# Folding the query weights early, in one burst, and keeping them in DRAM

## The chip, the cores and the metric

The kernel runs on one core of a Trainium2 chip. The metric is the time of one execution on the device in microseconds (us). A profiled execution also has a span, from its first to its last instruction, and a trace in which every instruction and transfer has its time.

## The reference

Two branches are computed from 2048 tokens of 512 features and mixed by a gate of each token.

```python
x = A_x                                         # 1 x 2048 x 512
g = sigmoid((x * gate_w).sum(-1))               # one gate per token
q, k, v = split(x @ wqkv)                       # 32 heads of 16
pq, pk = q @ w_phi[h], k @ w_phi[h]             # a 16 x 16 matrix per head
phi = concat([softmax(p), softmax(-p)])         # for pq and for pk
kv, z = phi_k^T v, sum over tokens of phi_k
a = (phi_q kv) / (phi_q z + 1e-6) @ wo
b = relu(x @ w1 + b1)^2 @ w2 + b2               # inner width 1792
out = g * a + (1 - g) * b
```

Since `pq = x @ (wq_h w_phi[h])`, the kernel multiplies each head's `wq` by its `w_phi` once (it folds them) and then projects the tokens with the folded weights. The same is done for the keys. The query fold is what is changed here.

## The kernel before

Tokens are cut into 4 blocks of 512 and each block into 4 chunks of 128. The feed-forward branch runs in two sweeps over the blocks. A sweep takes 7 of the 14 inner tiles of 128 features: for each block and inner tile one `up` (12 matmuls of 512 columns into one PSUM bank) and one `down` (12 matmuls, three into each of the four banks `d`). A float32 product is made of three matmuls with high and low parts (`mm3`, L76 to L78).

Everything else is hung between these matmuls by hand. `work_list` has 56 entries, and entry t owns the half steps 2t, 2t + 0.5, 2t + 1 and 2t + 1.5: before `up`, in its middle, before `down` and in its middle. So half steps stand six matmuls apart, and `at(slot, f, ...)` puts a function on one of them. The order that results is a priority: a planner lays the instructions of each engine out by it ahead of time, and `tc.high_priority(offset=AHEAD)` moves one forward in it, `tc.issue_after(i)` keeps one behind another on its engine, `behind()` keeps one behind the latest work of ScalarE and VectorE on `up`. On the chip each engine runs its own list in order and waits for semaphores.

What the change touches:

- `load_fold` (L141) loads `w_phi` and the four row tiles of `wqT` into five buffers of the pool `row`, which has six (`row`, L89). The same pool holds the token rows of the gate (`gate_load`, L265), the parts that the first sweep writes to DRAM at the end of each block (`part`, L898 to L910) and `kv_room`.
- `query_fold(half)` (L191) at half steps 51.5 and 53: 32 matmuls each, by `fold_block` (L166), over array tiles of 32 x 32 with 128 columns, into two PSUM banks; then VectorE transposes each bank in 32 x 32 blocks (`turned`, L174) and ScalarE and VectorE split the result into high and low parts (L63, L66), the weights `wq` of the projection `q` from half step 56.5 on.
- `tiles_fold` (L177) is the same fold for the keys, at half step 5.5.
- `pair_steps(p, s)` (L660) computes keys and values of two chunks by seven products, blocks 1 to 7 (`run(i)`, L680), with three sums of weights that are reloaded from DRAM (`wkeep`, `again`, L644) by ScalarE's queue. Pair 0 starts at s = 14, pair 1 at 18.5. Blocks 1, 6, 5, 3 write the bank X (pool `ps_e`), blocks 2, 7, 4 the bank Y, from the rotating list `banks`. `place` (L675, L677) takes the results out of X on ScalarE, out of Y on VectorE; `place7` is that of block 7, and block 4 adds to the same bank behind it. `phi` then makes the exponentials of a chunk.
- At that time `banks` holds two pools, which `up` and Y share. `ps_b` belongs to the sums `kv` from half step 21.5 on.

Of the kernel before, what the change touches and what calls it, by code (L numbers as in the profile page):

```python
# [7 lines left out]
F32 = mybir.dt.float32  # L8
F32R = mybir.dt.float32r
AF = mybir.ActivationFunctionType  # L10
# [5 lines left out]
P = 128  # L16
S, D, H, DH, F = 2048, 512, 32, 16, 1792
NK = D // P
# [10 lines left out]
AHEAD = 150  # L29
# [5 lines left out]
def tile_gated_mix(ctx: ExitStack, tc: tile.TileContext, xT, xn, wqT, wkT, wphi, wv, wo, w1, b1, w2, b2, gw, out):  # L35
    nc = tc.nc
# [8 lines left out]
    dram = pool("dram", 1, space=DRAM)  # L45
    ps_d = pool("ps_d", NC, space=PSUM)
    ps_a, ps_b, ps_e, ps_f = (pool(f"ps_{i}", 1, space=PSUM) for i in "abef")
    banks = [ps_a, ps_b, ps_e, ps_f]
    def used(p):
        banks.remove(p)  # L50
        banks.append(p)

    def bank(name):
        p = banks[0]
        used(p)
        return p.tile([P, 512], F32, tag="s", name=name)
# [4 lines left out]
    def split(src, hi, lo, ehi, elo):  # L61
        if ehi is nc.scalar:
            i = nc.scalar.activation(hi, src, AF.Copy)  # L63
        else:
            i = ehi.tensor_copy(hi, src)
        st["lo"] = elo.tensor_tensor(lo, src, hi.bitcast(F32), ALU.subtract)  # L66
        return i
# [21 lines left out]
    def row():  # L89
        return work.tile([P, D], F32, tag="row", name="row", bufs=6)  # L90
# [29 lines left out]
    st, up_w, down_w = {}, {}, {}  # L120
# [8 lines left out]
    nc.gpsimd.tensor_tensor(kvb, kvb, kvb, ALU.add)  # L129
    part = dram.tile([NB * NC, P, D], F32, name="part")  # L130
    wkeep = dram.tile([len(KEPT), 2, P, 2 * D], F32, name="wkeep")
    zrow = dram.tile([2 * D], F32, name="zrow")
    vext = [hold.tile([P, H * VW], F32, tag="vz", name=f"vext{i}") for i in range(NV)]
    heads = lambda v: v.rearrange("p (h v) -> p h v", v=VW)
# [28 lines left out]
    def fold_block(loaded, out, g, r, c):  # L163
        wph, *t = loaded
        rows, cols = slice(32 * r, 32 * r + 32), slice(32 * c, 32 * c + 32)
        return nc.tensor.matmul(out[cols, g * P:(g + 1) * P], wph[rows, g * P + 32 * r:g * P + 32 * r + 32],  # L166
                                t[g][rows, :].rearrange("p (k c q) -> p k c q", c=4, q=32)[:, :, c, :],
                                start=True, stop=True, skip_group_check=True)

    def turned(pss, half):  # L170
        tb = work.tile([P, 2, 4, NK, 32], F32, tag="tb", name="turned", bufs=2)
        for r in range(2):
            with tc.high_priority(offset=AHEAD):
                st["turned"] = nc.vector.transpose(tb[:, r].rearrange("p g k q -> p (g k q)"), pss[2 * half + r])  # L174
        return tb

# [11 lines left out]
                    nc.scalar.activation(dst[:, h, 0, :, 2 * half:2 * half + 2],  # L188
                                         tb[:, :, 2 * h:2 * h + 2, k].rearrange("p r g q -> p g r q"), AF.Copy)

    def query_fold(half):  # L191
        pss = {r: bank(f"fold{r}") for r in (2 * half, 2 * half + 1)}
        for g, c, r in [(g, c, r) for g in range(NK) for c in range(4) for r in pss]:
            with tc.issue_after(st["up"].ins):
                st["up"] = fold_block(st["wT"], pss[r], g, r, c)
        tb = turned(pss, half)
        part_ = lambda t: t.rearrange("p (g r f) -> p g r f", g=NK, f=32)[:, :, 2 * half:2 * half + 2, :]
        for k in range(NK):
            if not half:
                st.setdefault("wa", []).append(tuple(  # L200
                    wpool.tile([P, 512], F32R, tag=f"wa{hl}{k}", name=f"wq{hl}{k}") for hl in "hl"))
            hi, lo = st["wa"][k]
            split(tb[:, :, :, k].rearrange("p r g q -> p g r q"), part_(hi), part_(lo), nc.scalar, nc.vector)
# [84 lines left out]
    def e_tile(tag="e"):  # L288
        if tag == "tmp":
            return st["tmp"][1].rearrange("p (h t f) -> p h t f", t=2, f=DH)  # L290
        return work.tile([P, H, 2, DH], F32, tag="e", name="e", bufs=2)
# [343 lines left out]
    def again(p, i, j):  # L635
        if i not in KEPT:
            return nullcontext()
        step = 2 * KEPT.index(i) + j
        nxt, t = step + 3, st["slots"][step % 3]
        if nxt >= 6 and p == LASTP:  # L640
            return nullcontext()
        k, jj = KEPT[nxt % 6 // 2], nxt % 2
        st["W"][k, jj] = both(t)
        return tc.issue_after(nc.scalar.dma_start(t.bitcast(F32), wkeep[KEPT.index(k), jj]).ins)  # L644
# [15 lines left out]
    def pair_steps(p, s):  # L660
        b, c = ROWS[p]
        n, m = b * NC + c, b * NC + c + 2
        v = {}

        def place(t, half, src, other=None):
            i = 2 * p + (t == m)
            if ("e", t) not in v:
                v["e", t] = e_tile("tmp" if i % NV == NV - 1 else "e")
                v["v", t] = vext[i % NV]
            hs = slice(16 * half, 16 * half + 16)  # L670
            to = (v["e", t][:, hs, 0, :], heads(v["v", t])[:, hs, :DH])
            for o, cols in zip(to, halves):
                of = lambda z: z[:, cols].rearrange("p (h f) -> p h f", f=DH)
                if other is None:
                    read = nc.scalar.activation(o, of(src), AF.Copy)  # L675
                else:
                    read = nc.vector.tensor_tensor(o, of(other), of(src), ALU.add)  # L677
            return read

        def run(i):  # L680
            first, other = i in (1, 2, 7), "Y" if i in (2, 7, 4) else "X"
            if i == 1:
                if p == 0:
                    banks.remove(ps_e)
                v["X"] = ps_e.tile([P, 512], F32, tag="s", name="pX")
            elif first:
                v["bank"] = banks[0]
                v["Y"] = bank("pY")
            elif i == 4:
                used(v["bank"])  # L690
            block(v[other], p, i, first)
            with tc.high_priority(offset=AHEAD), again(p, i, 0):
                if i in (1, 6, 5):
                    v[i] = st["tmp"][0][:, 512 * (i == 6):512 * (i == 6) + 512]
                    read = nc.scalar.activation(v[i], v["X"], AF.Copy)  # L695
                elif i == 7:
                    return
                else:
                    t, half, u = {2: (n, 0, 1), 3: (n, 1, None), 4: (m, 0, 6)}[i]
                    read = place(t, half, v[other], v.get(u))  # L700
            with tc.issue_after(read.ins):
                again(p, i, 1)

        def place7():
            with tc.high_priority(offset=AHEAD):
                place(m, 1, v["Y"], v[5])

        def phi(t):
            e3, r = exps(e=v["e", t])
            with tc.high_priority(offset=AHEAD):  # L710
                v["phi", t] = scaled(e3, r)

        def kv():
            if p == 0:
                st["kv"] = ps_b.tile([P, 2 * P], F32, tag="s", name="kvps")
            later = kv_chunk(p == 0, False, st["kv"], v["phi", m], v["v", m])
            with tc.issue_after(later.ins):
                st["up"] = kv_chunk(False, p == LASTP, st["kv"], v["phi", n], v["v", n])

        at(s - 2 - (p > 0), sums_load, p)  # L720
        if p == 0:
            at(s - 2, sums_add, p)
        at(s - 1.5 if p else s - 0.5, sums, p)
        for off, i in zip((0, 1, 1.5, 2, 2.5, 3, 4), (1, 2, 6, 5, 7, 3, 4)):
            at(s + off, run, i)
        if p == LASTP:
            at(s + 4, banks.append, ps_e)
        at(s + 3, place7)
        at(s + 3, phi, n)
        at(s + 4, phi, m)  # L730
        at(s + 7.5 + (p == LASTP) * 1.5, kv)
# [55 lines left out]
    SL = 2 * NFH  # L787
    steps = {}

    def at(slot, f, *a):  # L790
        steps.setdefault(int(2 * slot) / 2, []).append(lambda: f(*a))
# [9 lines left out]
        at(14.5, joint_last, j)  # L801
    for b in range(NB):
        for c in range(NC):
            s = b * SL + 2.5 * c - 1 if b > 1 else 17.5 + c / 2 if b else max(5.5, 3.5 + 2 * c)
            if b != 1 or c < 2:
                at(s, gate_load, b * NC + c)
            at(s + (4.5 if b == 1 else 3), gate_chunk, b * NC + c)
        if c == NC - 1:
            at(s + 4.5 if b == 1 else s + 3, gates, b)
        s, late = ((4, 2), (19.5, 1), (22, 2.5), (36, 2))[b]  # L810
        at(s, x_load, b + 1)
        for k in range(NK):
            at(s + late + k / 2, x_split, b + 1, k)
    for p in range(NB * NC // 2):
        pair_steps(p, 14 + 4.5 * p)
    base = (NB - 1) * SL
    at(49, do_wT, wqT)
    at(51.5, query_fold, 0)
    at(53, query_fold, 1)
    for k in range(NK):  # L820
        at(base + 8.5 + k, wo_load, k)
        at(base + 10 + k, wo_split, k)
# [10 lines left out]
    for p in range(NB * NC // 2):  # L833
        n, s = 2 * p, 56.5 + 6 * p
        q, late = divmod(n, NC)[0], p == NB * NC // 2 - 1
# [122 lines left out]
```

## Time and profile before

| | |
|---|---|
| median of 3 runs | 506.2 us (506.01 to 506.32) |
| the profiled execution | 506.27 us |
| its span | 504.5 us, 9559 instructions |
| busy: PE, PEld, DVE, ACT, POOL | 499.7, 403.9, 404.7, 259.9, 88.1 us |
| granted TensorE clock | 0.999 |
| DMA | 76.13 MB, mean 151 GB/s |

PE is TensorE's matmuls, PEld its weight loads, DVE VectorE, ACT ScalarE, POOL GpSimd, SP the engine that only issues transfers. A row of a timeline has the start in us, the duration in us, engine, line of the kernel, instruction, output <- inputs with shapes, and how many were merged; in brackets the idle time before it and what ended it. Matmuls overlap: 512 columns last 0.39 us each but start 0.23 us apart. A row of a line or tile has the shortest, median and longest duration in ns, and first and last start. A row of windows has the stretch, its length, the busy time and number of instructions for PE, PEld and further engines, and at its end the granted clock, the share of DMA in use and GB/s; where it is asked for one line alone, it counts only that line's instructions. "DMA to landing" is the time from a transfer's issue to the arrival of its last byte.

### The profile page before, as it was taken

What the parts mean: (1) busy time and instruction counts of PE and PEld (TensorE: products, weight loads), DVE (VectorE), ACT (ScalarE), POOL (GpSimd) and SP (SyncE); (2) the same over time, 40 slices, a digit from 0 to 9 for tenths busy, and PEclk for the clock granted to TensorE, in tenths of its full rate; (3) what the DMA queues carried; (4) which work ended last, traced back from release to release, by engine and by line L of the source; (5) the groups of instructions that cost most, each with busy time, mean ns of one, the idle gap of its engine ahead of it and who ended that gap; (6) DMA issues with size and microseconds to landing.
All of it is one profiled execution on the core that took longest, in us unless ns stands there. A gap on an engine that the chain in (4) does not pass through costs nothing.

```text
span 504.5 us, 9559 instructions
## 1 busy us (share of the span) xinstructions
PE 499.7 (99%) x3616; PEld 403.9 (80%) x3616; DVE 404.7 (80%) x680; ACT 259.9 (52%) x470; POOL 88.1 (17%) x103
## 2 busy tenths in 40 slices
PE   8999999999999999999999999999999999999997
PEld 5878788888888888888788878788787878788776
DVE  5569957799785969796988989897979796897724
ACT  4887655466263474453793644454455353333540
POOL 1000151204510025000012140212222221112200
PEclk9999999999999999999999999999999999999999
DMA  8858587666854578762167131324212221041112
GB/s 263 285 197 279 184 315 215 215 216 233 295 187 156 180 225 309 261 218 75 43 182 280 39 109 47 101 71 138 54 31 90 71 88 44 6 136 51 36 29 83
DMA packets 45830, 76.13 MB, mean 151 GB/s; under 512 B 6869, under 2 KB 23001, under 8 KB 45785
## 3 DMA queue, kind: packets, MB, share of 16 engines
q1 hardware_dynamic: 36072, 41.78, 26.5%
q10 hardware_dynamic: 6768, 23.79, 13.6%
q0 software_dynamic: 2944, 9.96, 5.4%
q8 instruction: 28, 0.46, 0.3%
q14 instruction: 18, 0.14, 0.1%
HBM read 57.68 MB, written 11.54 MB: 137 GB/s over the span
## 4 chain that ended last, share of the span: by engine, by line
PE 93%; DMA 3%; DVE 2%; issue 1%; ACT 1%; SPq 0%; ACTq 0%; DVEq 0%
PE d L76 9%; PE d L77 9%; PE d L78 9%; PE u L76 9%; PE u L77 9%; PE u L78 9%; PE pX L656 3%; PE q L78 3%; PE att L78 3%; PE att L76 3%; PE q L76 3%; PE att L77 3%; PE q L77 3%; PE pX L658 3%; PE pX L657 3%; PE pY L656 2%
## 5 line engine op out<-in xcount | busy, mean ns | idle before, releaser
L425 ACT ACTIVATE r<-u,b1c 128x512 f32<-128x512 f32 x56 | 38.5, 687 | 110.1 <-PE u L78 108.3
L76 PE MATMUL d<-w2h,hh 128*128 128x512 f32 x222 | 86.8, 391 | 0.0
L77 PE MATMUL d<-w2l,hh 128*128 128x512 f32 x222 | 86.4, 389 | 0.0
L78 PE MATMUL d<-w2h,hl 128*128 128x512 f32 x222 | 86.4, 389 | 0.0
L76 PE MATMUL u<-xh,w1h 128*128 128x512 f32 x212 | 83.5, 394 | 0.0
L77 PE MATMUL u<-xl,w1h 128*128 128x512 f32 x212 | 82.6, 390 | 0.0
L78 PE MATMUL u<-xh,w1l 128*128 128x512 f32 x212 | 82.5, 389 | 0.0
L337 POOL TENSOR_TENSOR ez<-e,z 128x512 f32<-128x512 f32 x32 | 43.0, 1366 | 164.1 <-ACT e L313 164.1
L66 DVE TENSOR_TENSOR hl<-r,hh 128x512 fp32r<-128x512 f32 x56 | 37.9, 677 | 22.9 <-ACT hh L63 22.9
L76 PEld LDWEIGHTS d<-w2h,hh 128*128 128x128 f32 x222 | 41.7, 188 | 9.6 <-issue 1.0
L76 PEld LDWEIGHTS u<-xh,w1h 128*128 128x128 f32 x212 | 39.8, 188 | 11.4 <-issue 2.9
L78 PEld LDWEIGHTS d<-w2h,hl 128*128 128x128 f32 x222 | 41.7, 188 | 8.7
L77 PEld LDWEIGHTS d<-w2l,hh 128*128 128x128 f32 x222 | 41.7, 188 | 8.5
L78 PEld LDWEIGHTS u<-xh,w1l 128*128 128x128 f32 x212 | 39.8, 188 | 8.4
L77 PEld LDWEIGHTS u<-xl,w1h 128*128 128x128 f32 x212 | 39.8, 188 | 8.0
L313 ACT ACTIVATE e<-e 128x1024 f32<-128x1024 f32 x27 | 28.6, 1060 | 32.5 <-DVE e L311 32.1
L295 DVE TENSOR_REDUCE sm<-e 128x64 f32<-128x1024 f32 x27 | 32.8, 1215 | 10.8 <-ACT e L313 10.8
L63 ACT ACTIVATE hh<-r 128x512 fp32r<-128x512 f32 x56 | 35.1, 627 | 1.0
L427 ACT ACTIVATE r<-r 128x512 f32<-128x512 f32 x56 | 34.9, 624 | 0.7
L378 ACT ACTIVATE phiT<-tb 32x256 f32<-32x256 f32 x64 | 26.4, 413 | 8.8 <-DVE tb L363 7.9
L695 ACT ACTIVATE tmp<-pX 128x512 f32<-128x512 f32 x24 | 14.4, 598 | 29.7 <-PE pX L658 24.7
L347 DVE TENSOR_REDUCE dz<-ez 128x64 f32<-128x1024 f32 x16 | 19.4, 1212 | 11.7 <-POOL ez L337 11.7
(181 smaller groups left out, 981.4 us busy)
## 6 DMA issues: line engine op xcount, KB each, us to landing
sloto<-wkeep ACTq DMA_DIRECT2D x30, 512.0 KB, 4.3
in<-in_xT SPq DMA_DIRECT2D x42, 256.0 KB, 4.4
slotez<-wkeep ACTq DMA_DIRECT2D x15, 512.0 KB, 6.0
phiT<-tb SPq DMA_DIRECT2D x192, 32.0 KB, 1.8
in<-in_w SPq DMA_DIRECT2D x23, 256.0 KB, 3.3
part<-row POOLq DMA_DIRECT2D x16, 256.0 KB, 5.2
row<-part SPq DMA_DIRECT2D x16, 256.0 KB, 3.2
out<-row SPq DMA_DIRECT2D x15, 256.0 KB, 2.2
```

What stands on the lines that cost most here:

```text
L63: i = nc.scalar.activation(hi, src, AF.Copy)
L66: st["lo"] = elo.tensor_tensor(lo, src, hi.bitcast(F32), ALU.subtract)
L76: nc.tensor.matmul(o, ah[:, sa], bh[:, sb], start=first, stop=False)
L77: nc.tensor.matmul(o, ah[:, sa], bl[:, sb], start=False, stop=False)
L78: return nc.tensor.matmul(o, al[:, sa], bh[:, sb], start=False, stop=last)
L295: nc.vector.tensor_reduce(sm, e3, AX.X, ALU.add)
L313: nc.scalar.activation(ef, ef, AF.Exp)
L337: nc.gpsimd.tensor_tensor(ez[:, hs, :], e3[:, hs, :], zbc[half], ALU.mult)
L378: nc.scalar.activation(dst, src, AF.Copy)
L425: st["relu"] = nc.scalar.activation(r, ps, AF.Relu, bias=b1c[:, fc:fc + 1])
L427: nc.scalar.activation(r, r, AF.Square)
L656: nc.tensor.matmul(ps, h, wh, start=first and j == 0, stop=False, skip_group_check=True)
```

## The change

The five loads go to half step 16. At 17.5 one burst of 16 matmuls of 512 columns, one for each pair of row group r and column group g of the array, folds all query weights into four banks: the two of `banks`, `ps_e` and `ps_b`. ScalarE copies each bank into a `row` buffer, and 16 transfers of 64 KB from SP's queue put them into the DRAM tensor `qkeep`. At half step 49 four loads of 256 KB bring them back, and at 51.5 and 53 `query_turn` does what `query_fold` did after its matmuls, with the transposes reading SBUF and not moved forward in priority. For the banks, pair 0 runs block 4 at half step 17 (18 before) and `place7` at 16.5 (17 before). The gate loads of block 1 go from 17.5 to 18.5, with their products.

```diff
+    qkeep = dram.tile([4, 4, 32, NK, P], F32, name="qkeep")
...
-    def turned(pss, half):
+    def turned(pss, half, ahead=True):
         tb = work.tile([P, 2, 4, NK, 32], F32, tag="tb", name="turned", bufs=2)
         for r in range(2):
-            with tc.high_priority(offset=AHEAD):
+            with tc.high_priority(offset=AHEAD) if ahead else nullcontext():
                 st["turned"] = nc.vector.transpose(tb[:, r].rearrange("p g k q -> p (g k q)"), pss[2 * half + r])
         return tb
...
-    def query_fold(half):
-        pss = {r: bank(f"fold{r}") for r in (2 * half, 2 * half + 1)}
-        for g, c, r in [(g, c, r) for g in range(NK) for c in range(4) for r in pss]:
-            with tc.issue_after(st["up"].ins):
-                st["up"] = fold_block(st["wT"], pss[r], g, r, c)
-        tb = turned(pss, half)
+    def query_fold():
+        pss = [p.tile([P, 512], F32, tag="s", name=f"fold{r}") for r, p in enumerate((banks[0], ps_e, banks[1], ps_b))]
+        wph, *t = st["wT"]
+        for g in range(NK):
+            for r in range(4):
+                rows, cols = slice(32 * r, 32 * r + 32), slice(32 * g, 32 * g + 32)
+                with tc.issue_after(st["up"].ins):
+                    st["up"] = nc.tensor.matmul(
+                        pss[r][cols, :], wph[rows, g * P + 32 * r:g * P + 32 * r + 32],
+                        t[g][rows, :].rearrange("p (k c q) -> p c k q", c=4, q=32),
+                        start=True, stop=True, skip_group_check=True)
+        for r in range(4):
+            t = row()
+            with tc.high_priority(offset=AHEAD):
+                st["folded"] = nc.scalar.activation(t, pss[r], AF.Copy)
+            for g in range(NK):
+                nc.sync.dma_start(qkeep[r, :, :, g, :].rearrange("c f x -> f c x"),
+                                  t[32 * g:32 * g + 32, :].rearrange("f (c x) -> f c x", c=4))
+
+    def query_load():
+        st["wT"] = [row() for _ in range(4)]
+        for r, t in enumerate(st["wT"]):
+            nc.sync.dma_start(t, qkeep[r].rearrange("c f g x -> (c f) (g x)"))
+
+    def query_turn(half):
+        tb = turned(st["wT"], half, False)
...
-        for off, i in zip((0, 1, 1.5, 2, 2.5, 3, 4), (1, 2, 6, 5, 7, 3, 4)):
+        for off, i in zip((0, 1, 1.5, 2, 2.5, 3, 4 if p else 3), (1, 2, 6, 5, 7, 3, 4)):
             at(s + off, run, i)
...
-        at(s + 3, place7)
+        at(s + (3 if p else 2.5), place7)
...
-            s = b * SL + 2.5 * c - 1 if b > 1 else 17.5 + c / 2 if b else max(5.5, 3.5 + 2 * c)
+            s = b * SL + 2.5 * c - 1 if b > 1 else 18.5 + c / 2 if b else max(5.5, 3.5 + 2 * c)
...
-    at(49, do_wT, wqT)
-    at(51.5, query_fold, 0)
-    at(53, query_fold, 1)
+    at(16, do_wT, wqT)
+    at(17.5, query_fold)
+    at(49, query_load)
+    at(51.5, query_turn, 0)
+    at(53, query_turn, 1)
```

## The prediction

> **What bounds the kernel now.** I read the page's head and chain first, then TensorE's timeline round the work that the change touches, then ScalarE, VectorE and DMA at the step where it goes.
>
> ```profile
> span 504.5 us, 9559 instructions
> PE 499.7 (99%) x3616; PEld 403.9 (80%) x3616; DVE 404.7 (80%) x680; ACT 259.9 (52%) x470; POOL 88.1 (17%) x103
> PE 93%; DMA 3%; DVE 2%; issue 1%; ACT 1%; SPq 0%; ACTq 0%; DVEq 0%
> 66.14 0.39 PE L76 MATMUL u<-xh,w1h 128*128 128x512 f32 x1
> 71.58 0.39 PE L656 MATMUL pY<-w,xh 128*128 128x512 f32 x1
> 57.45 0.40 PE L76 MATMUL u<-xh,w1h 128*128 128x512 f32 x1
> 57.96 0.50 PE L656 MATMUL pX<-slotez,sh 128*128 128x512 f32 x1
> ```
>
> TensorE is busy 99% of the span and is 93% of the chain, so time is what TensorE issues plus the places where its stream breaks. From 66.14 to 71.58 there are 24 matmuls: 5.44 us, 0.227 us each; that is the beat. The step from 57.45 to 57.96 misses it by 0.28 us: one of the few waits. A change gains here only by taking time out of TensorE's stream, and loses by every wait that it puts into it. Other engines' work is free as long as nobody in that stream waits for it.
>
> **What is removed.** Two query folds at half steps 51.5 and 53.
>
> ```profile
> 240.52 0.39 PE L78 MATMUL d<-w2h,hl 128*128 128x512 f32 x1
> 240.84 1.15 PE L166 MATMUL fold<-row 32*32 32x128 f32 x64
> 241.92 0.50 PE L76 MATMUL d<-w2h,hh 128*128 128x512 f32 x1
> 242.26 0.39 PE L77 MATMUL d<-w2l,hh 128*128 128x512 f32 x1
> 246.23 1.15 PE L166 MATMUL fold<-row 32*32 32x128 f32 x64
> ```
>
> The stream goes from 240.52 to 242.26 with two ordinary matmuls in it: 1.74 - 2 x 0.227 = 1.29 us for the burst with its switch in and out. The second burst has the same 64 passes and the same 1.15 us, so I put it at 1.29 too: 2.58 us leave the stream. (32 matmuls show 64 passes: float32 goes through twice.)
>
> **What is added on TensorE.** One burst of 16 matmuls, 32 passes of 512 columns, two in each of 16 array tiles. No such pass is in the trace; these rows bound it.
>
> ```profile
> L166 PE MATMUL fold<-row x256: 265/268/293, 26.6 to 247.1; 32*32 32x128 f32 x128
> L389 PE MATMUL num<-phiT,kvb x256: 376/376/400, 296.6 to 488.3; 64*32 64x256 f32 x128
> 296.28 0.39 PE L78 MATMUL u<-xh,w1l 128*128 128x512 f32 x1
> ...
> 296.59 1.09 PE L389 MATMUL num<-phiT,kvb 64*32 64x256 f32 x32
> 297.62 0.50 PE L76 MATMUL u<-xh,w1h 128*128 128x512 f32 x1
> 297.95 0.40 PE L77 MATMUL u<-xl,w1h 128*128 128x512 f32 x1
> 26.61 1.90 PE L166 MATMUL fold<-row 32*32 32x128 f32 x128
> 26.60:26.73 0.13, 0.12 (x16) 0.12 (x31) 1.00 0.68 205
> 246.20:246.34 0.14, 0.11 (x8) 0.11 (x16) 1.00 0.00 0
> ```
>
> A pass takes 268 ns with 128 columns and 376 ns with 256: 108 ns for each 128 columns, so 432 ns of streaming for 512. The key fold of the start, over 16 tiles, starts 16 passes in its first 0.13 us; the query fold, over 8 tiles, starts 8 in 0.14 us. So every tile streams at the same time as the others, and one tile's two passes are what follows each other. Streaming in the new burst is 2 x 432 = 0.86 us. The old query burst has 8 x 108 = 0.86 us of streaming in each tile and costs 1.29, so 0.43 us for the switches and the staggered starts; num has 4 x 216 = 0.86 us and costs 1.67 - 0.45 = 1.22, so 0.36. Lower bound of the new burst: 0.86 + 0.43 = 1.29 us. Upper bound: its passes arrive only as fast as in the key fold's whole burst, (1.90 - 0.27) / 127 = 12.8 ns apart, so the last tile starts 31 x 12.8 = 0.40 us late: 0.86 + 0.36 + 0.40 = 1.62 us. I take the upper one, since a bank that the third matmul writes comes free only just before the burst (below), so few passes can be queued ahead. Gain on TensorE: 2.58 - 1.62 = 0.96 us, and 1.29 at best.
>
> A rule of the Trainium skill speaks against this ("TensorE: Matmul & The Clock Gate", Part 3: Packing small matmuls): matmuls start and end strictly in program order. By it a tile's second pass would hold up the next tile. The two window rows, 16 and 8 starts at once, say otherwise for passes of this kind; what it would give is a rival below.
>
> **Moved earlier: place7 and block 4 of pair 0.** Block 4 ran at half step 18 from 71.58 on. It now follows block 3 at 17, so the burst is due 24 beats after 66.14 (six of `up`, block 3, block 4, six of `down`): at 71.58, where block 4 was.
>
> ```profile
> 70.08 0.68 DVE L309 TENSOR_REDUCE mn<-e 128x32 f32<-128x512 f32 x1
> 70.79 0.69 DVE L310 TENSOR_TENSOR e<-mn,e 128x512 f32<-128x512 f32 x1
> 73.14 0.42 DVE L677 TENSOR_TENSOR e<-tmp,pY 128x256 f32<-128x256 f32 x1 [0.93 <-PE pY L658]
> 66.40 0.42 DVE L677 TENSOR_TENSOR e<-tmp,pY 128x256 f32<-128x256 f32 x1 [2.67 <-ACT hh L63]
> ```
>
> place7's additions ran at 66.4 already, and block 4 now comes 12 beats after 66.14, at 68.86: nothing waits. Block 4's two additions of 0.42 us can follow mn at 70.8 and free the Y bank at about 71.5: in time by a tenth. If they came only after the next two steps of phi(n) (2 x 0.69), TensorE would stand for up to 1.4 us. I take 0, because these additions are issued ahead of phi(n) by priority. The X bank was last written by block 3, six beats earlier, and kv's bank is not in use yet.
>
> **Moved earlier: five loads (weights) to half step 16.** They need five of the six `row` buffers. Four hold block 0's parts then.
>
> ```profile
> 52.00:56.00 4.00, 4.00 (x19) 3.32 (x18) 4.00 (x11) 1.48 (x3) 0.93 (x2) 1.00 0.64 256
> 68.00:72.00 4.00, 4.00 (x19) 3.34 (x18) 2.45 (x4) 2.20 (x5) 2.46 (x5) 1.00 0.73 263
> 72.00:76.00 4.00, 4.00 (x19) 3.30 (x19) 3.07 (x7) 2.24 (x4) 0.00 (x0) 1.00 0.77 304
> L910 POOL DMA_DIRECT2D part<-row x1: 542/542/542, 63.4 to 63.4; - x1
> DMA to landing us min/median/max: 4.8/4.8/4.8
> L145 SPq DMA_DIRECT2D row<-in_wqT x4: 328/338/1360, 199.7 to 236.2; - x4
> DMA to landing us min/median/max: 3.1/4.4/8.6
> L265 POOL DMA_DIRECT2D row<-in_xn x2: 544/553/562, 68.3 to 68.9; - x2
> 56.11 0.60 ACT L695 ACTIVATE tmp<-pX 128x512 f32<-128x512 f32 x1 [1.47 <-DMA wkeep<-spare]
> 80.20 0.62 ACT L63 ACTIVATE xh<-in 128x512 fp32r<-128x512 f32 x1
> 81.10 0.39 PE L656 MATMUL pX<-slotez,sh 128*128 128x512 f32 x1
> ```
>
> Two loads find free rows before; the other three follow the first three part stores. The third store starts at 63.4 and lands 4.8 us later, at 68.2; the same load before took 3.1 to 8.6 us, so the last weights land at 71.3 to 76.8, 72.6 by the median. Its four matmuls are the last of the burst and due at about 72.0 (71.58 and three quarters of the paced starts). I take no wait, since the DMA share there is 0.73 and the two gate loads (xn) that ran at 68.3 and 68.9 now wait for rows themselves, until the burst frees them at about 73. Those two stand on GpSimd's queue, and the loads of token block 2 behind them; ScalarE first splits one of these at 80.20, so 4 to 5 us of delay leave some cover and cost nothing.
>
> **Added after the burst.** Four copies on ScalarE: the 0.60 us row above, 2.4 us from about 73 on. ScalarE has 1.8 and 1.76 us free in the two windows 68 to 76, and what stands behind them on ScalarE (the sums of pair 1) is first used at 81.10. The next `up` needs the first copy alone, one `down` group (1.36 us) after the burst: hidden. If that cover went, up to 2.4 us would show.
>
> ```profile
> 245.85 1.73 SPq L243 DMA_DIRECT2D in<-in_wo  x4
> 45.60 44.88 SPq L611 DMA_DIRECT2D in<-in_xT  x3
> L66 DVE TENSOR_TENSOR wql<-turned,wqh x8: 392/416/420, 248.1 to 254.2; 128x256 fp32r<-128x256 f32 x8
> 258.42 0.39 PE L76 MATMUL q<-wqh,xh 128*128 128x512 f32 x1
> ```
>
> Sixteen stores of 64 KB on SP: the nearest row, four pieces of 64 KB, issues one in 0.43 us: 6.9 us, 73 to 80, on a queue that issues three transfers between 45.6 and 90.5. They are hidden, since whatever SP does next comes after them; their 1 MB shares the DMA with the reloads of `wkeep`, at a share of 0.77. At half step 49 four loads replace five. The four transposes remain but no longer go ahead of other VectorE work; the last query weight was done by 254.7 and is used at 258.42, a cover of 3.7 us. I cost all this at 0.
>
> **Sum.** 506.27 us (the profiled execution; its span of 504.5 and 1.8 around it) - 2.58 + 1.62 + 0 = 505.31. The median of the runs, 506.20, is 0.07 lower, so the forecast is 505.2 us, 504.9 with the lower bound of the burst.
>
> **Rivals.**
> 1. The early loads collide. ScalarE waited 1.47 us at 56.11 for the store of `spare` to land, and TensorE's gap at 57.96 hangs on that queue. If the rows that block 0's last gate chunks free just before then are the ones used, a 256 KB load runs beside that store. At the 256 GB/s of 52 to 56 it takes 1.0 us; from nothing to 1.0 us goes into the gap. Time 505.2 to 506.2, 505.7 in the middle. The Trainium skill ("DMA: Bandwidth & Descriptors", Issuing engines are not separate DMA queues) says that transfers of all issuing engines share the same 16 DMA engines; no row here shows these two together.
> 2. The burst waits for its last weights, or is cut up by it (the slower side). At a landing of 76.8 it is 4.8 us late and the time 510.0; from 1.0 us late the gain is gone, from 2.0 us the kernel is slower by 0.2%. If the planned order puts other matmuls between, each further piece costs at least the switch and two streams, 0.36 + 0.86 = 1.2 us: in two pieces 506.5, in three 507.7. For it: five of six buffers, and stores in between. Against: the median landing is 0.6 us late at most.
> 3. Passes go in order: 17 x 0.432 + 0.36 = 7.7 us for the burst, 506.2 - 2.58 + 7.7 = 511.3. The starts of 16 and 8 at once are against it.
>
> **How the numbers follow.** A change of 0.2% (1.0 us) is about what a measurement of this kernel tells from none. Forecast (whole burst, all hidden, 504.8 to 505.5): 0.52, of which 0.40 beyond 0.2%. Rival 1: 0.26, of which 0.03 beyond it. Rival 2: 0.20, of which 0.02 within 0.2%. Rival 3: 0.02. So faster 0.43, same 0.37, slower 0.20. The range of 8 in 10 is 504.7 to 507.2: below, the best burst with a little of the old gaps gone; above, a burst in two to three pieces or 2 us late.
>
> **What would show it.** Right: no fold at 240 and 246; one group of 32 passes near 72 us, 1.3 to 1.6 us out of the beat; the step at 57.96 as before; later work earlier by 1 us after half step 53. Wrong: the group in several pieces with `d` or `u` between; TensorE released by a DMA of `row`; a longer gap at 58; `u` waiting for a fold copy on ScalarE; q waiting for `wql` after 254.

## The result and the profile after

The changed kernel takes 515.7 us (median of 5 runs, 514.8 to 515.9) against 506.2 before: ratio 1.018, 95% interval 1.017 to 1.020. It is slower by 9.5 us where 1.0 us less was forecast. The profiled execution after is the fastest of the five: 514.78 us, a span of 513.0. One execution is left out of the range and the ratio given for its kernel below: one of the five of experiment 8 took 1287.9 us at a granted clock of 1.00, and no trace of it was kept.

The head of the page after, with the granted clock, the DMA and the chain:

```profile
span 513.0 us, 9412 instructions
PE 502.6 (98%) x3520; PEld 404.1 (79%) x3520; DVE 407.7 (79%) x680; ACT 261.9 (51%) x474; POOL 86.0 (17%) x103
PEclk9999999999999999999999979999999999999999
PE 88%; DMA 4%; SPq 3%; DVE 3%; issue 1%; ACT 1%; ACTq 0%; DVEq 0%
```

There are fewer instructions, yet TensorE is busy 3 us longer and the granted clock has one weak slice, the 24th of 40, which is about 295 to 308 us. The chain has lost 5 points of PE to DMA, SP's queue and VectorE: TensorE now waits where it did not. TensorE's timeline after shows where, in order of time:

```profile
58.47 0.42 PE L679 MATMUL pX<-slotez,sl 128*128 128x512 f32 x1
60.65 0.50 PE L677 MATMUL pX<-sloto,sh 128*128 128x512 f32 x1 [1.75 <-DMA sloto<-wkeep]
...
73.04 0.39 PE L78 MATMUL d<-w2h,hl 128*128 128x512 f32 x1
73.36 1.38 PE L199 MATMUL fold<-row 32*32 32x512 f32 x32
74.66 0.50 PE L76 MATMUL d<-w2h,hh 128*128 128x512 f32 x1
75.00 0.39 PE L77 MATMUL d<-w2l,hh 128*128 128x512 f32 x1
...
75.93 0.40 PE L78 MATMUL d<-w2h,hl 128*128 128x512 f32 x1
76.87 0.50 PE L76 MATMUL u<-xh,w1h 128*128 128x512 f32 x1 [0.55 <-ACT row L206]
...
260.12 0.39 PE L76 MATMUL q<-wqh,xh 128*128 128x512 f32 x1
...
298.36 0.59 PE L410 MATMUL num<-phiT,kvb 64*32 64x256 f32 x2
301.91 1.96 PE L410 MATMUL num<-phiT,kvb 64*32 64x256 f32 x30 [2.96 <-DMA phiT<-tb]
303.79 0.79 PE L76 MATMUL u<-xh,w1h 128*128 128x512 f32 x1
304.38 0.63 PE L77 MATMUL u<-xl,w1h 128*128 128x512 f32 x1
```

Read each against the beat of 0.227 us (a row's start minus the start of the row above it):

- Near 58, a wait for the reload of `sloto`. All gaps of this place together are 1.76 us longer than before.
- The burst: 75.00 - 73.04 = 1.96 for the burst and two ordinary matmuls, so 1.51 us. Forecast: 1.29 to 1.62.
- `u` waits for the first fold copy: 0.72 + 0.11 = 0.83 us out of the beat.
- `num`, the first product of the first query pair, has two passes and then waits 2.96 us for `phiT`. Its other 30 passes take 1.96 us, where the whole of it took 1.09 before, and the matmuls behind stand 0.43 us apart instead of 0.227. Counted in the beat, this place is 6.54 us longer than before.

The windows of the kernel after, whose third number from the right is the granted clock, say what the 0.43 us are:

```profile
core 0: us, PE busy (x) PEld busy (x) DVE busy (x) ACT busy (x) POOL busy (x), PEclk, DMA share, GB/s
301.90:303.80 1.90, 1.89 (x31) 0.73 (x31) 1.83 (x3) 0.00 (x0) 1.35 (x2) 0.50 0.70 207
303.80:308.20 4.40, 4.40 (x16) 3.46 (x11) 4.37 (x6) 2.53 (x5) 0.00 (x0) 0.50 0.46 160
```

For some 6 us behind the wait TensorE ran at half clock. The whole account: -2.57 (old bursts) + 1.51 + 1.76 + 0.83 + 6.54 + 0.23 (a short wait near 133 that the kernel before doesn't have) = 8.3, and the two profiled executions are 514.78 - 506.27 = 8.5 apart.

Why is `phiT` late? VectorE transposes each chunk into `tb`, and SP sends 24 pieces, one after the other, for the two chunks of a pair. SP's rows of the kernel before:

```profile
279.32 15.39 SPq L372 DMA_DIRECT2D phiT<-tb  x24
```

and of the kernel after:

```profile
284.65 15.87 SPq L393 DMA_DIRECT2D phiT<-tb  x24
```

The queue needs the same 15.4 to 15.9 us, but begins 5.3 us later, while `q` and `num` begin only 1.7 and 1.8 us later (258.42 and 296.59 before, 260.12 and 298.36 after). A chunk's chain on VectorE has these steps: `mx`, `mn` and two `e` (maximum, minimum and the differences for the softmax), `sm` and `r` (the sum and its reciprocal), `dz` and `den` (the denominator), `w`, `e<-e,w` (the scaling) and `tb` (the transpose). VectorE's timeline before, the first chunk's `den`, `e<-e,w` and `tb` and the second chunk's `mx`:

```profile
272.75 0.35 DVE L352 RECIPROCAL den<-den 128x32 f32<-128x32 f32 x1
273.02 0.63 DVE L308 TENSOR_REDUCE mx<-q 128x32 f32<-128x512 f32 x1
...
275.75 1.23 DVE L318 TENSOR_TENSOR e<-e,w 128x1024 f32<-128x1024 f32 x1
...
278.02 1.24 DVE L363 STREAM_TRANSPOSE tb<-e 128x1024 f32<-128x1024 f32 x1
```

and after:

```profile
273.74 0.68 DVE L329 TENSOR_REDUCE mx<-q 128x32 f32<-128x512 f32 x1
...
275.94 0.68 DVE L332 TENSOR_TENSOR e<-q,mx 128x512 f32<-128x512 f32 x1
...
277.97 0.35 DVE L373 RECIPROCAL den<-den 128x32 f32<-128x32 f32 x1
...
282.09 1.21 DVE L339 TENSOR_TENSOR e<-e,w 128x1024 f32<-128x1024 f32 x1
...
283.36 1.23 DVE L384 STREAM_TRANSPOSE tb<-e 128x1024 f32<-128x1024 f32 x1
```

In the kernel after, the four softmax steps of the second chunk stand ahead of the first chunk's `dz` and `den` (two of them ahead of its `r` too), and `sm` and `dz` of the second chunk are let in before the first chunk's `e<-e,w`. No step's own work grew but one (last section). The first transpose starts 283.36 - 260.12 = 23.2 us after `q`, against 278.02 - 258.42 = 19.6. Before, the last piece was issued at about 294.1 and lands 1.8 us later, at 296.0; the bulk of `num` was due at 296.6. The cover was 0.6 us, and 3.6 us were taken from it.

### The profile page after: what moved, and what is told of

It reads as the page before. It is cut to its first block, busy times and chain, and to the rows that moved or that the text cites. A ratio compares the mean times of both kernels' runs of the same rounds, so it can differ in the third digit from the quotient of the medians.

```text
span 513.0 us, 9412 instructions
## 1 busy us (share of the span) xinstructions
PE 502.6 (98%) x3520; PEld 404.1 (79%) x3520; DVE 407.7 (79%) x680; ACT 261.9 (51%) x474; POOL 86.0 (17%) x103
## 4 chain that ended last, share of the span: by engine, by line
PE 88%; DMA 4%; SPq 3%; DVE 3%; issue 1%; ACT 1%; ACTq 0%; DVEq 0%
PE d L76 9%; PE u L76 9%; PE d L78 9%; PE d L77 9%; PE u L78 8%; PE u L77 8%; PE pX L677 3%; PE att L78 3%; PE att L77 3%; PE att L76 3%; PE pX L679 3%; SPq L393 3%; PE pX L678 3%; PE q L78 3%; PE q L76 3%; PE q L77 3%
```

## The experiments

My theory after this reading: the loss has three causes, in this order. VectorE's order round the first queries, which the planner chose anew because work had gone from the program; an early load beside a reload at 58; the order of copies and exponential on ScalarE. The rivals were that the kept weights' own DMA traffic, or their late transposes, made `phiT` late.

### 1. VectorE's order put back

```diff
-    def exps(ps=None, e=None, late=False):
+    def exps(ps=None, e=None, late=False, den=None):
...
-        with tc.high_priority(offset=AHEAD):
+        with tc.high_priority(offset=AHEAD), tc.issue_after(den.ins) if den else nullcontext():
...
-        e3, r = exps(ps, late=n == 3)
+        e3, r = exps(ps, late=n == 3, den=(None, st.get(("den", 0)), st.get("tb"))[n] if n < 3 else None)
...
-        nc.vector.reciprocal(den, den)
+        st["den", n] = nc.vector.reciprocal(den, den)
...
-        nc.vector.transpose(tb, phi)
+        st["tb"] = nc.vector.transpose(tb, phi)
```

> The changed kernel with two orders written out on VectorE and nothing else: the softmax steps of the second query chunk come after the reciprocal of den of the first, those of the third after the second chunk's transpose, as the kernel before had them. TensorE's order is the same as in the changed kernel. Theory (VectorE's order): in the changed kernel the first transpose tb ran at 283.36, and the 24 pieces phiT<-tb, one each 0.63 us on SP, end so late that num waits 2.96 us and then runs at a granted clock of 0.50; with the order of before the first transpose comes at about 280, the last piece lands before num, and the 6.5 us lost there go: 515.7 - 6.5 = 509.2 us, 508.2 to 510.2, granted clock 0.9 or more round num. Rival (DMA): the pieces are late because the DMA engines carry the kept query weights and other loads: nothing changes, 515 to 516. Rival (late query weights, because their transposes no longer go ahead): q itself is late, so 515 to 516.

Measured: 510.7 us (509.7 to 512.7), 0.5 us above the range that I expected; the profiled execution 509.65, ratio to before 1.008 (1.005 to 1.011). TensorE at `num`:

```profile
298.59 0.62 PE L410 MATMUL num<-phiT,kvb 64*32 64x256 f32 x2
299.49 1.09 PE L410 MATMUL num<-phiT,kvb 64*32 64x256 f32 x30 [0.28 <-DMA phiT<-tb]
```

The wait is down from 2.96 to 0.28 us, the passes take 1.09 us again, and the mean granted clock is 1.0. Nothing else was touched, so 5 us of the 9.5 hang on this order. The transfers and the late transposes of the kept weights are as in the kernel after, so both rivals fall. The first transpose comes at 281.24, 20.8 us after `q`, not yet 19.6: `w2l` and `hl` still stand ahead of it. The waits at 58 (2.1 us here) and 76 (0.7) remain, and with them the distance to 506.

### 2. Two early loads earlier still

```diff
-    at(16, do_wT, wqT)
+    at(12, first_two)
+    at(16, other_three)
```

`first_two` loads `wphi` and `wqT[:, 0]`, `other_three` the rest of `wqT`.

> The changed kernel with two of the five early loads (wphi and the first of wqT) asked for at half step 12 instead of 16, ahead of the rows of block 0's parts, so that they are on SP's queue ahead of the second pair of rows; the other three stay at 16. Theory (the load beside the reload): in the changed kernel the reload sloto<-wkeep issued at 55.45 took 5.15 us, beside a load of wqT issued 0.04 us earlier, against 3.21 us before, and TensorE stood 1.76 us longer round 58; with both loads landed before 52 the reload takes 3.2 to 3.5 us and the 1.76 us go: 515.7 - 1.8 = 513.9 us, 513.4 to 514.4. Rival (the reload is slowed by the stores of the kept weights alone): the reload still takes about 5 us and the time stays at 515.2 to 516. The wait of num at 298 and the half clock after it stay in both.

The transfers issued between 54.5 and 56.5, with their time to landing, in the kernel after:

```profile
sloto<-wkeep ACTq DMA_DIRECT2D x1, 512.0 KB, 5.2
row<-in_wqT SPq DMA_DIRECT2D x1, 256.0 KB, 5.0
```

In the kernel before the same reload took 3.2 us; in this experiment, with no load beside it:

```profile
sloto<-wkeep ACTq DMA_DIRECT2D x1, 512.0 KB, 3.6
```

TensorE has no gap at 58 at all. So the mechanism of the theory holds: the reload was slow because a load ran beside it. But the time did not follow: 518.0 us (515.7 to 519.9). The burst, reached earlier, now waits twice for its last weights:

```profile
71.10 1.32 PE L199 MATMUL fold<-row 32*32 32x512 f32 x16
73.18 1.06 PE L199 MATMUL fold<-row 32*32 32x512 f32 x8 [0.76 <-DMA row<-in_wqT]
75.31 1.06 PE L199 MATMUL fold<-row 32*32 32x512 f32 x8 [1.07 <-DMA row<-in_wqT]
```

Its place costs over 5 us here. The wait at 58 had been hiding a second one, for the three loads that need rows of the part stores. But hiding is only a part of it: the burst was due 2.3 us earlier than in the kernel after (71.1 and 73.4), and the last of these loads, issued at 67.6 and 67.5, also landed 2.8 us later (75.3 and 72.5).

### 3. The fold copies ahead of the exponential

```diff
-        nc.scalar.activation(ef, ef, AF.Exp)
+        with tc.issue_after(after.ins) if after else nullcontext():
+            nc.scalar.activation(ef, ef, AF.Exp)
...
-            e3, r = exps(e=v["e", t])
+            e3, r = exps(e=v["e", t], after=st["folded"] if p == 0 else None)
...
-        at(s + 3, phi, n)
+        at(s + (3 if p else 4), phi, n)
```

> The changed kernel with one order changed on ScalarE: in pair 0 the exponential of phi(n) comes after the four copies of the fold's banks, and phi(n) is asked for half a step pair later. Theory (ScalarE's order): u waited for the first copy at 76.07 because the exponential, which itself waited 1.65 us for VectorE, stood ahead of it on ScalarE; the 0.83 us there go: 515.7 - 0.8 = 514.9 us, 514.4 to 515.2. Rival (the copies are late because the banks themselves are done late, or the later phi(n) makes kv wait): no gain, 515.4 to 516.5.

ScalarE's rows of the kernel after show what was to be mended: the exponential waits for VectorE, and the copies stand behind it.

```profile
75.28 1.06 ACT L334 ACTIVATE e<-e 128x1024 f32<-128x1024 f32 x1 [1.65 <-DVE e L332]
76.24 2.04 ACT L206 ACTIVATE row<-fold 128x512 f32<-128x512 f32 x4
```

Measured: 514.95 us (513.8 to 517.8), which tells nothing from 515.7. In the trace `u` no longer waits behind the burst, but in this execution the last weights landed late and the burst itself stood:

```profile
73.37 1.11 PE L199 MATMUL fold<-row 32*32 32x512 f32 x24
76.52 1.06 PE L199 MATMUL fold<-row 32*32 32x512 f32 x8 [2.04 <-DMA row<-in_wqT]
```

A later burst gives the copies more time as well, so this run alone doesn't settle the 0.8 us. The eighth has no wait there with an undisturbed burst.

### 4. Two idle bursts of the old form put back

```diff
+    def old_burst(half):
+        pss = {r: bank(f"fold{r}") for r in (2 * half, 2 * half + 1)}
+        loaded = [st["wT"][0]] + st["wT"]
+        for g, c, r in [(g, c, r) for g in range(NK) for c in range(4) for r in pss]:
+            with tc.issue_after(st["up"].ins):
+                st["up"] = fold_block(loaded, pss[r], g, r, c)
...
+    at(51.5, old_burst, 0)
     at(51.5, query_turn, 0)
+    at(53, old_burst, 1)
     at(53, query_turn, 1)
```

> The changed kernel with two bursts of the old form (each 32 products of 128 columns) put back at half steps 51.5 and 53; they read the loaded rows and nobody reads what they write. What they cost TensorE is 2 x 1.29 us by the profile of before. The planned order of VectorE round the first queries becomes that of before by this alone. Theory (VectorE's order, which the planner changed because 2.6 us of TensorE's work went): num no longer waits: 515.7 + 2.6 - 6.5 = 511.8 us, 511 to 512.8, although TensorE has more to do. Rival (DMA or late query weights): 515.7 + 2.6 = 518.3, 517.5 to 519.

Measured: 513.5 us (511.4 to 515.4), above the 511 to 512.8 that I expected and below the rival's 517.5; the profiled execution 512.37. The median of the changed kernel was 515.7, so with 2.6 us more work on TensorE the kernel was about 2 us faster, though single runs of the two overlap. `num` has all its passes in one group and full clock:

```profile
302.15 1.38 PE L417 MATMUL num<-phiT,kvb 64*32 64x256 f32 x32
```

VectorE's order at the first queries is that of the kernel before in this build:

```profile
278.79 0.35 DVE L380 RECIPROCAL den<-den 128x32 f32<-128x32 f32 x1
279.06 0.63 DVE L336 TENSOR_REDUCE mx<-q 128x32 f32<-128x512 f32 x1
...
284.06 1.23 DVE L391 STREAM_TRANSPOSE tb<-e 128x1024 f32<-128x1024 f32 x1
```

The first transpose starts 20.1 us after `q` at 263.98. So with everything else of the change in place, it is the missing folds that tip the planner to the other order. Whether they would tip it without the rest of the change no run shows, nor what in the planner's reckoning does it.

### 5 and 10. The changed kernel again

> The changed kernel once more, unchanged, beside the runs of the next three. In the single experiments the burst itself waited up to 2.4 us for its last weights, which it did not do in the profile of the changed kernel, so I want its spread. Theory (the burst's wait depends on how the transfers between 60 and 76 us happen to share the DMA engines): the median is 515 to 517, the single runs lie up to 3 us apart, the wait of num at 298 with the half clock is there each time, the wait in the burst only sometimes. Rival (only the edits of those experiments made the burst wait): 515.2 to 516, as before, with no wait inside the burst.

> The changed kernel a third time, on the same chip as the run before it. Theory (each wait of TensorE of 1.7 us or more may bring on a stretch of half clock, and does so in some runs): waits at 58 and at num as in its two other profiles, 514.5 to 517, granted clock below 0.997; each stretch of half clock behind a wait of at least 1.7 us and nowhere else. Rival (the half clock has its own times): a stretch of half clock with no wait ahead of it.

Measured: 515.8 (514.7 to 517.4) and 514.7 (513.0 to 519.1), ratios to before 1.019 (1.017 to 1.022) and 1.019 (1.015 to 1.023): the loss is stable. A part of what changes from run to run is the clock, whose mean lies between 0.990 and 0.999 in these eight runs; it is not all, since two of them at 0.993 took 515.1 and 519.1 us. In the first of the two a wait of 1.5 us at 58 was already followed by half clock (0.62 over 60 to 64 us):

```profile
60.00:64.00 4.00, 3.66 (x10) 2.89 (x11) 3.25 (x6) 1.82 (x3) 1.12 (x3) 0.62 0.93 323
```

In the second the wait at `num` was there in full, and no half clock came:

```profile
303.00 1.09 PE L410 MATMUL num<-phiT,kvb 64*32 64x256 f32 x30 [2.97 <-DMA phiT<-tb]
...
304.36 0.40 PE L77 MATMUL u<-xl,w1h 128*128 128x512 f32 x1
```

That execution took 512.96 us. My expectation that each profile would show it was wrong; no stretch of half clock was seen without such a wait right ahead of it. The burst's place cost 1.75 us in the first, where the last weights landed 0.5 us after its start, and 1.51 in the second; in experiments 2, 3 and 6 it waited 1 us and more.

### 6. num half a step later

```diff
-        at(s + 10 - late, do_n, p)
+        at(s + (10 - late if p else 10.5), do_n, p)
```

> The changed kernel with num of the first query pair asked for half a step later: six matmuls of up now stand ahead of it on TensorE instead of behind it; nothing else is moved. Theory (a wait of 3.1 us plus a half clock that this wait brings on): the pieces land when they did, so the wait shrinks by the six matmuls, 3.1 - 1.36 = 1.7 us, and as the 1.9 us wait at 58.6 in the changed kernel was followed by full beats, no half clock follows: num's burst is back at 1.2 us and the 11 matmuls at 0.43 us are back at 0.227. Saved: 1.36 + 0.87 + 2.2 = 4.4 us, 515.7 - 4.4 = 511.3, 510.3 to 512.3. Rival (the half clock belongs to something else at that time and not to the wait): only 1.36 us is saved, 514.3, and the granted clock still shows 0.50 behind num.

Measured: 513.7 us (511.5 to 516.4), where I expected 510.3 to 512.3. In the profiled execution, 511.54, the wait shrank as forecast and no half clock followed:

```profile
302.95 1.09 PE L410 MATMUL num<-phiT,kvb 64*32 64x256 f32 x30 [1.80 <-DMA phiT<-tb]
```

The other runs were 511.9, 515.5 and 516.4, the last two with a mean clock of 0.993, as in the profile of the kernel after. So the consumer's side gains the 1.4 us. Why two runs were slower no trace shows; their clock suggests half clock again, somewhere (the last section has more on when it comes).

### 7. The moves alone, on the kernel before

```diff
-        for off, i in zip((0, 1, 1.5, 2, 2.5, 3, 4), (1, 2, 6, 5, 7, 3, 4)):
+        for off, i in zip((0, 1, 1.5, 2, 2.5, 3, 4 if p else 3), (1, 2, 6, 5, 7, 3, 4)):
...
-        at(s + 3, place7)
+        at(s + (3 if p else 2.5), place7)
...
-            s = b * SL + 2.5 * c - 1 if b > 1 else 17.5 + c / 2 if b else max(5.5, 3.5 + 2 * c)
+            s = b * SL + 2.5 * c - 1 if b > 1 else 18.5 + c / 2 if b else max(5.5, 3.5 + 2 * c)
```

> The kernel before with only the moves of the change: block 4 of pair 0 half a step pair earlier, place7 of pair 0 at its new place, the gate loads of token block 1 one half step later. The folds stay as they were. Theory (these moves cost nothing, as the prediction had it): 506.2 to 506.7, no wait of TensorE over 0.3 us that the kernel before has not. Rival (the earlier block 4 or the later gate loads upset VectorE or the loads behind them): 507 or more, with a wait between 66 and 90 us.

Measured: 506.4 us against 506.3, ratio 1.0006 (0.9994 to 1.0019). The moves of pair 0 cost nothing.

### 8, 9 and 12. All waits mended

The eighth has experiments 1 and 3 and places all weights but the last where they need no part store. One goes into `vext[2]`, whose ones are written again behind the burst (the `memset`):

```diff
+    def query_weight(i):
+        t = vext[2][:, :D] if i == 2 else st["tmp"][1][:, D:] if i == 3 else row()
+        nc.sync.dma_start(t, wqT[:, i - 1, :] if i else wphi)
+        st.setdefault("early", []).append(t)
+        st["wT"] = st["early"]
...
+        nc.gpsimd.memset(heads(vext[2])[:, :, DH:VW], 1.0)
...
-    at(16, do_wT, wqT)
+    for i in range(1 + NK):
+        at((12, 12, 12, 13, 16)[i], query_weight, i)
```

> The changed kernel with the three waits mended together: VectorE's order as in the first experiment, the copies ahead of the exponential as in the third, and the early loads placed where they wait for no part store: wphi and the first of wqT in rows at half step 12, the second in the third vext buffer, which is idle until pair 1 (its ones are written again after the burst), the third in the half of tmp that is dead after half step 9, and only the last in a row that a part store frees. Theory (three waits, and the burst waits because its last weights queue behind the part stores): 515.7 - 6.5 - 1.8 - 0.8 = 506.6, 505.5 to 507.5, with no wait over 0.6 us at 58, in the burst, at 76 or at num. Rival (the DMA engines are full from 60 to 92 us, so a transfer moved only makes another late): the waits move to other blocks of pairs 0 and 1 and the time is 508 to 511.

Measured: 508.1 us (507.2 to 508.4), ratio 1.003 (1.002 to 1.005), above the 505.5 to 507.5 that I expected and at the lower end of the rival's range. The waits in the burst and at 76 are gone, and the place at 58 costs 0.3 us more than in the kernel before. The burst, with all its weights and banks there:

```profile
71.33 0.39 PE L78 MATMUL d<-w2h,hl 128*128 128x512 f32 x1
...
73.06 0.40 PE L77 MATMUL d<-w2l,hh 128*128 128x512 f32 x1
```

73.06 - 71.33 - 2 x 0.227 = 1.28 us, the forecast's lower bound of 1.29. So the exchange on TensorE is worth 2.57 - 1.28 = 1.29 us, and it is there. What stands against it are waits that the kernel before doesn't have:

```profile
141.80 0.50 PE L78 MATMUL u<-xh,w1l 128*128 128x512 f32 x1 [0.88 <-issue]
...
298.10 1.09 PE L412 MATMUL num<-phiT,kvb 64*32 64x256 f32 x30 [0.48 <-ACT e L336]
```

`num` is still 1.1 us long in the beat (the first transpose comes 20.9 us after `q`; the row names ScalarE, but the last piece was issued at 296.1 and landed at 298.0), 1.04 us at 141 are ended by nothing that the trace shows, and 0.5 us at 130 hang on VectorE. Without these 2.6 us the execution would, by this sum, be at 505.5; no run shows it.

The ninth adds the edit of the sixth:

> The kernel with the three waits mended (the eighth experiment) and, on top of it, num of the first query pair half a step later as in the sixth; nothing else. In the eighth, num still waited 0.63 us for its last pieces. Theory (cover of the first query pair's pieces): six matmuls, 1.36 us, ahead of num cover that wait whole: 508.1 - 0.6 = 507.5, 506.8 to 508.2, no wait at num; that is still about 1 us above the kernel before, since the waits at 130 (VectorE) and 140 (no releaser shown) remain, and the gain of the change on TensorE is only 1.1 to 1.4 us. Rival (num later makes the products behind it late, att or the next copies): 508 to 509.5.

Measured: 508.5 us, ratio 1.004 (1.002 to 1.006). `num` no longer waits, but `att` behind it does, as the rival said:

```profile
305.09 0.50 PE L78 MATMUL att<-woh,o 128*128 128x512 f32 x1 [1.45 <-DVE o L66]
```

The twelfth adds to the eighth a priority on the first chunk's chain:

```diff
-        phi = q_phi(n)
+        with tc.high_priority(offset=AHEAD) if n < 1 else nullcontext():
+            phi = q_phi(n)
...
-        st["diag", n] = transposed(phi, st["pt", n // 2], c % 2)
+        with tc.high_priority(offset=AHEAD) if n < 1 else nullcontext():
+            st["diag", n] = transposed(phi, st["pt", n // 2], c % 2)
```

> The kernel with the three waits mended (the eighth experiment), and on VectorE the steps from den to the transpose of the first query chunk also ahead by priority, so that only mx, mn, e, e of the second chunk stand between them. In the eighth the first transpose came 20.9 us after q, against 19.6 in the kernel before. Theory (cover of the pieces): the first transpose moves up by about 1.9 us, the second stays, the last piece lands about 0.5 us earlier and num's wait falls from 1.1 to about 0.6 us: 508.1 - 0.5 = 507.6, 506.6 to 508.3; still no gain on the kernel before. Rival (the second chunk's chain becomes the later one): 508 to 509, num waits 1 us or more.

Measured: 509.3 us, ratio 1.005 (1.004 to 1.006). The first transpose moves up to 276.25, 19.1 us after `q`, but the second stays at 287.15, 30.0 us after `q` (27.5 before), and now SP's last twelve pieces wait for it: `num` idles 1.34 us. The rival held, with a time a little above its 508 to 509. No version here beats the kernel before.

### 11. The kernel before, with VectorE's order as after

```diff
-        at(s, do_phi, NB + q, n, n % NC)
+        at(s + (0 if p else 2), do_phi, NB + q, n, n % NC)
...
-            nc.vector.tensor_tensor(e[:, :, 0, :], pv, bc(mx), ALU.subtract)
+            st["sub"] = nc.vector.tensor_tensor(e[:, :, 0, :], pv, bc(mx), ALU.subtract)
...
-        nc.vector.tensor_tensor(dz, dz, r, ALU.mult)
+        with tc.issue_after(st["sub"].ins) if n == 0 else nullcontext():
+            nc.vector.tensor_tensor(dz, dz, r, ALU.mult)
```

> The kernel before with nothing of the change in it, but with VectorE's order round the first two query chunks as the changed kernel has it: the softmax steps of the second query chunk (mx, mn, e, e) come ahead of den, w and the transpose of the first. TensorE's order is that of the kernel before. Theory (VectorE's order alone makes the loss at num): the first transpose starts 22.5 to 23.5 us after q instead of 19.6, the last of the 24 pieces lands 2.5 to 3.5 us after num is due, num waits that long, and in some runs a stretch of half clock adds about 3 us: 506.3 + 2.5 to 3.5 = 508.8 to 509.8 without the half clock, 511.5 to 513 with it. Rival (the loss needs the kept weights, their transfers or their late transposes): 506 to 506.8, num waits under 0.6 us.

Measured: 509.9 us (509.7 to 510.3) against 506.8 beside it, ratio 1.007 (1.004 to 1.009).

```profile
298.50 1.31 PE L390 MATMUL num<-phiT,kvb 64*32 64x256 f32 x30 [1.65 <-DMA phiT<-tb]
...
300.33 0.63 PE L77 MATMUL u<-xl,w1h 128*128 128x512 f32 x1
```

The first transpose starts at 280.44, 22.4 us after `q`, the wait and the half clock behind it appear, and there is no kept weight, no early load and no missing fold in this kernel. So the order alone brings the loss, of 3 us here. It is smaller than in the kernel after, and the wait is shorter than I had expected (1.65 us for 2.5 to 3.5): the transpose comes 0.9 us earlier, and the order is not wholly that of the kernel after, as the second chunk's `dz` stands behind the first chunk's `e<-e,w` here. Two of the four runs had a mean clock of 0.999 and 1.000 and took 509.7 and 510.1 us all the same, so half clock alone does not explain the 3 us.

## Why the prediction was wrong

- **The removed bursts** left the stream as said: 1.28 us each in the kernel before, 2.57 together, and 1.29 each where experiment 4 puts them back. **The new burst** cost 1.51 us in the profile, within 1.29 to 1.62, and 1.28 with nothing late; its first 16 passes start within 0.1 us in the eighth experiment and within 0.34 in the kernel after, and the third rival (passes in order, 7.7 us) is refuted. The sum on TensorE was right: -1.1 us against the -0.96 that I took.
- **The step that failed** is "Other engines' work is free as long as nobody in that stream waits for it", together with "I cost all this at 0" for what comes after half step 51.5. I looked at the last query weight (used without a wait in the trace after, as forecast) and at nothing behind it. The chain from `q` over VectorE to the 24 pieces and `num` had 0.6 us of cover in the profile before, and VectorE's order along it is not written in the code but chosen by the planner. Taking TensorE's work out changed the choice: 6.5 us of the 8.5, of which some 3 are half clock (in experiment 10 the same wait without half clock costs 3.7 us). No rival named it.
- **"The next `up` needs the first copy alone, one `down` group (1.36 us) after the burst: hidden"** failed for 0.83 us. ScalarE did come free, but the exponential of `phi(n)`, which waits for VectorE, stood ahead of the copy. I had counted ScalarE's free time and not its order.
- **Rival 1** had the right place and the wrong partner and size. The store of `spare` was not disturbed in the profile after (3.65 us, 3.79 before; in experiment 1 it took 4.59); the reload of `sloto`, issued 0.04 us after a load of `wqT`, took 5.2 us for 3.2, and TensorE lost 1.76 us where at most 1.0 was allowed. The Trainium skill ("DMA: Bandwidth & Descriptors", Issuing engines are not separate DMA queues) says that transfers of different issuing engines interleave on the same 16 DMA engines; the trace agrees, 3.6 us without the load and 5.2 with it.
- **Rival 2**, the burst waiting for its last weights, was given a landing of 72.6 by the median. In the profile after the last landed at 72.5 and the burst was due late enough, at 73.4, thanks to the wait at 58. In experiments 2, 3 and 6 it waited 1 to 4 us. It was a real mechanism, hidden behind the other one in the run that was to be explained.
- **The moves** cost nothing, as forecast (experiment 7). The sixteen stores and four loads of the kept weights put no wait of their own on TensorE in the profile after. In experiment 10, the same kernel, TensorE waited 1.07 us at 89, while the stores ran; whether they caused it is open.

## What to carry to other kernels

Where a planner orders the engines, a cut in one engine's work is an edit of every engine's order: list the chains that meet the bound engine in the stage behind the cut, with the cover of each, and expect the one with the least to break. A wait on TensorE is dear beyond its length, since it can bring on a stretch of half clock. And when one wait is mended, ask what it was hiding: three mended waits gave back 7.6 of the 9.5 us here, and the mendings of experiments 2, 9 and 12 each brought another wait into sight.

## What was not expected of the hardware

- Waits far under 3 us can be followed by half clock: 1.5 us (experiment 5, at 58) and 1.65 us (experiment 11) were, 1.75 us (at 58 in the kernel after), 1.80 (experiment 6) and 2.97 (experiment 10) were not. The granted clock is then 0.50, for 3.4 us (experiment 11) or 6.8 (the kernel after, 301.4 to 308.2). The Trainium skill ("TensorE: Matmul & The Clock Gate", What's actually happening) puts the return to half rate behind an idle window of about 3.4 us; the runs show it after half of that, and not each time.
- The length of a wait does not sort these cases, but its place does for most. In every trace here the changes of the granted clock lie whole multiples of 3.41 us apart (in experiment 5 at 60.94, 64.35, 303.29 and 310.11). I counted the time without a matmul in stretches of that length, laid end to end from these changes. Four stretches had 1.9 us or more (at `num` in the kernel after and in experiments 2, 3 and 5), and half clock began behind each of them. With 1.5 to 1.7 us it began behind two of five, and with less behind none. The 2.97 us of experiment 10 lay across two stretches, 1.46 us in one and 1.52 in the other; the 1.80 us of experiment 6 were 1.39 and 0.41. Why 1.53 us in a stretch (experiment 5) was enough and 1.70 (experiment 3, at 58) was not stays open.
- A short VectorE step can take five times as long. The line of `den<-den,gate` in the kernel after, shortest, median and longest in ns:

```profile
L374 DVE TENSOR_SCALAR den<-den,gate x16: 224/241/1236, 279.3 to 482.2; 128x32 f32<-128x32 f32 x16
```

The two long ones, 1.20 and 1.24 us, both begin while GpSimd runs a product `ez` and end 0.04 us after it (280.51 and 280.47, 302.06 and 302.02). Experiments 5, 6 and 10 have the same two, with the same ends; in the kernel before and experiments 1, 4, 8 and 11 no such step begins inside an `ez`, and none is long. That the two share something is likely and was not tested apart. The first lies in the chain to `num`, but it can be no more than 0.5 of its 3.6 us of delay: the second chunk's `dz`, which stands ahead of `e<-e,w` and starts at 280.97, needs the `ez` that ends at 280.47.
- Open: the wait with no releaser at the same matmul near 141 us, 0.2 to 1.3 us in most of the experiments, absent from the profiles before and after.
